# Power instead of Newton steps for the norms on GpSimd, norm rows and shifted copies moved between queues, the first X spectrum with a negated table, in an H3 convolution and SwiGLU kernel

## The chip, the cores and the metric

The kernel runs on one core of a Trainium2 chip. The core has five engines that run side by side, each working through its own queue in order: TensorE (PE, matrix products into PSUM; its weight loads are listed apart as PEld), VectorE (DVE), ScalarE (ACT), GpSimd (POOL) and SyncE (SP, which here only issues transfers). SP, ACT and POOL can issue DMAs; 16 DMA engines move the data. The metric is the device time of one execution in microseconds (us), the median of several runs. Lower is better.

## The reference

The input has 2048 positions of 640 channels. The part that matters:

```python
x = A_q
q = layernorm(x)                                   # no gain, no bias, eps 1e-5
k_shift[s] = sum_{t<4} k[s - t] * shift_k[:, t]    # four taps per channel
kv = k_shift * v
y = causal convolution of kv with ssm_k, by FFT    # length 2048, per channel
y = y + kv * ssm_D
h = x + q * y
n = layernorm(h)
out = h + (silu(n @ w_gate) * (n @ w_up)) @ w_down # 640 -> 1728 -> 640
```

Tiles are bf16; PSUM and the statistics of the norms are fp32.

## The kernel before, in words

**Tiling.** The 2048 positions are cut into four blocks (numbers 0 to 3) of 512. A block is a tile of 128 partitions by 4 rows by 640 channels; row r holds the positions 4p+r. The convolution is block by block: `spectrum` turns a block of kv into its spectrum X and a block of the filter into G by products with a table of cosines and sines (`WF`); `window` joins neighbouring G into H; `mac` adds up X_i * H_(j-i) on DVE; `inverse` goes back with the table `WI` and applies the first norm, the product with y and the sum h. `turn_h` applies the second norm and transposes h (hT). `ffn` then does the feed-forward part of the block: seven groups of gate and up columns (540 matmuls of 128x512 in all four blocks, line 1017), SiLU and product, then the down projection (416 matmuls of mostly 128x320, line 1105).

**The spectrum.** In `transform`, the cosine table of the even rows (0, 2) and of the odd rows (1, 3) give two halves E and O. Plain way: PE makes E, an engine copies 2E out of PSUM, PE adds O, an engine copies E+O, and DVE subtracts to get E-O (line 409). With a name in `DIRECT`, PE makes all four rows at once, then adds -2 times the odd rows from a second, negated table (`minus`), and both halves are copied out of PSUM; DVE subtracts nothing.

**The norms.** ACT sums x and x squared (lines 791, 749; four instructions each of 128x640). `norm` turns these into a mean and 1/sqrt(variance) on tiles of 128x4. On DVE that is ten short instructions, with a cubic polynomial behind a bit trick. On GpSimd it is fourteen, with the bit trick and two Newton steps (lines 767, 758, 759, 770, 779 to 782 twice, 758, 759). ln1 is the norm of x (result used on the way out of `inverse`, line 802), ln2 that of h (used in `turn_h`; the rows are applied by ACT at line 802 or DVE at line 799).

**k with four taps.** For blocks 1 to 3, k is loaded transposed into one tile T (four transposing DMAs), and then three copies inside T (line 562: put 0, put 1, put 2) make shifted halves, each 64 partitions by 5 by 512; put 1 and put 2 both come behind put 0. Two matmuls with pairs of taps then do what four did (line 640). All puts are DMAs, on SP's queue or on GpSimd's.

**Order.** Nothing is ordered by the hardware. `plan.add` numbers every operation in the order in which the code makes it, and the list `ORDER` gives these numbers in the order in which they are issued; each engine so gets a fixed queue. A negative number (~n) takes the operation's alternative: for an eviction from PSUM, DVE instead of ACT; for a load or put, GpSimd's queue instead of SP's. `SLOTS` says how many buffers there are of each sort: four pairs of PSUM banks (`ps`), eleven of 128x2560 bf16 (`big`) that loads, spectra halves, hT and FFN weights share, five rows (`row`), and so on. An operation waits for its data and for the last use of its buffer. The times in the `plan.add` calls were used for making the list; on the chip they do nothing.

Lines that the text below speaks of: 374 spectrum matmuls, 363 and 366 their evictions on ACT and DVE, 409 the subtraction E-O, 470/472 transposes of the filter and their eviction, 516/517 window, 562 puts, 711 to 739 `mac`, 818/821/887/900 the steps of `inverse`, 873 its matmuls, 921/923 transposes of h and their eviction, 954 FFN weight loads, 1007/1009 copies of the up half and SiLU, 1011 product, 1111 output rows of a block.

Of the kernel before, what the change touches and what calls it, by code (L numbers as in the profile page):

```python
# [26 lines left out]
NEWTON = ((1.68191274, 0.70395035), (1.50000037, 0.50000005))  # L27
# [11 lines left out]
DIRECT = ('G0',)  # L39
ACTLN = 0  # L40
ACTKV = 0
ACTLN2 = (0, 2)
LN1DVE = (2,)
LN2POOL = ()
# [14 lines left out]
FFN4 = True  # L59
# [8 lines left out]
TWONS = 640  # L68
TW = PAD + BLK
CUTS = ("X0", "G0", "m", "i")  # L70
ORDER = [
# [36 lines left out]
SLOTS = {'S': 8, 'kT': 0, 'tT': 1, 'row': 5, 'ps': 4, 'sm': 6, 'big': 11, 'sg': 0, 'co': 2}  # L108
HOME = {t: "big" for t in ("scr", "x", "ld", "t4", "hT", "wgu")} | {"o": "row", "ps_c": "ps", "ps_f": "ps"}
# [38 lines left out]
class Plan:  # L148
# [34 lines left out]
    def moved(self, eng, nbytes, packet, fn, reads=(), writes=()):  # L183
        n = nbytes / packet
        op = self.add(eng, 1000.0 if eng in ("turn", "aturn") else n * self.TOOK[packet] / 16 * (2.1 if eng == "add" else 1.0), fn, reads, writes)
        op.packets = 0 if eng == "add" else n
        return op
# [25 lines left out]
def kernel(ctx: ExitStack, tc: tile.TileContext, A_q, A_k, A_v, A_shift_k, A_ssm_k, A_ssm_D, B_x,  # L213
# [28 lines left out]
    def ap(b):  # L242
        if b.tag != "big":
            return b.ap if b.tag is None else place[b.tag][b.at]
        t = place["big"][b.at]
        return t if b.kind == "ld" else t.rearrange("p (k n) -> p k n", k=KT if b.kind in ("hT", "wgu") else R)
# [17 lines left out]
    def load(nbytes, packet, fn, w, r=(), other=None):  # L264
        op = plan.moved("sp", nbytes, packet, fn, r, w)
        if other:
            op.other = ("pld", op.ns, other)
        return op
# [33 lines left out]
    diag = fixed([P, KT * 4, P], BF16, "diag")  # L302
# [14 lines left out]
    def of_t(*atoms):  # L317
        return (T, frozenset(atoms))
    wd = fixed([P, NCH, D], BF16, "wd")
    tail = fixed([P, BLK], BF16, "tail")  # L320

# [223 lines left out]
    def load_two(j):  # L545
# [14 lines left out]
        def put(r, w, to, src):  # L560
            def by(q):
                return lambda: q.dma_start(out=to(), in_=src())
            load(H2 * KT * 1024, 1024, by(nc.sync), w, r, other=by(nc.gpsimd) if "T" in GLOAD else None)
        uppers = [("A", a, 1) for a in range(R)]
        put([of_t(*uppers)], [of_t("B0", *FIRSTS)], lambda: t()[0:H2, 1, :, PAD:TW], lambda: t()[H2:P, 0, :, PAD:TW])
        put([of_t("B0", "Bh")], [of_t("B1", *FIRSTS)], lambda: t()[H2:P, 1, :, PAD - 2:TW], lambda: t()[0:H2, 1, :, PAD - 3:TW - 1])
        put([of_t("Ah", *[("A", a, 0) for a in range(R)])], [of_t(*uppers)], lambda: t()[H2:P, 0, :, PAD - 2:TW], lambda: t()[0:H2, 0, :, PAD - 3:TW - 1])
# [184 lines left out]
    def norm(s, v, mean=None, bias=False, rs=range(R)):  # L752
# [11 lines left out]
        def go():  # L764
            if mean:
                fused(sm(s, 2), sm(s, 0), 1.0 / D, sm(mean, 2), ALU.mult, ALU.add)
            v.tensor_mul(sm(s, 6), sm(s, 2), sm(s, 2))
            fused(sm(s, 3), sm(s, 1), EPS, sm(s, 6), ALU.add, ALU.subtract)

            v.tensor_scalar(sm(s, 4).bitcast(I32), sm(s, 3).bitcast(I32), -0.5, float(0x5F165000 if v is nc.vector else 0x5F1FFFF9), op0=ALU.mult, op1=ALU.add)  # L770
            if v is nc.vector:
# [11 lines left out]
            if bias:  # L783
                fused(sm(s, 5), sm(s, 2), -1.0, sm(s, 4), ALU.mult, ALU.mult)
# [537 lines left out]
```

## Time and profile before

| | |
|---|---|
| median of 3 runs | 264.18 us (263.42 to 265.51) |
| the profiled execution | 264.92 us, its span 263.2 us, mean granted PE clock 0.994 |
| busy in the span | PE 252.7 us (96%), DVE 202.6 (77%), ACT 173.3 (66%), POOL 91.5 (35%) |
| 128x512 matmuls (line 1017) | 540, 121.1 us busy |
| 128x320 and the like, down projection (line 1105) | 416, 60.3 us busy |
| 128x320, spectra (line 374) | 256, 43.6 us busy |
| steps of the norm on GpSimd (lines 758 to 782) | 42 in three norms |

The span runs from the first to the last instruction; 1.7 us of the execution lie outside it. The busy time of PE is the union of its matmuls with modelled ends, so short waits hide in it; the start of one matmul to the start of the next tells more.

### The profile page before, as it was taken

The page shows a single profiled execution, that of the slowest core. Times are in us where ns is not written, and L with a number is a line of the kernel's source. Part 1 is how long each engine was busy: PE and PEld are TensorE (multiplying, and loading weights), DVE is VectorE, ACT ScalarE, POOL GpSimd, SP SyncE. Part 2 cuts the span into 40 slices and gives each one's busy share as a digit, 9 for nine tenths or more (in the row PEclk, how much of TensorE's full clock was granted, in tenths as well). Part 3 has the DMA queues.
Part 4 walks back from the last instruction along what each step waited for, and adds up shares of the span by engine and source line. Part 5 has one row for each costly group of instructions (what it writes and reads, how often), then busy time and mean ns, then how long its engine had stood idle before and what let it go on. Part 6 is the DMA issues. An engine that isn't in the chain of part 4 may idle for free.

```text
span 263.2 us, 4751 instructions
## 1 busy us (share of the span) xinstructions
PE 252.7 (96%) x1818; PEld 154.7 (59%) x1818; DVE 202.6 (77%) x288; ACT 173.3 (66%) x294; POOL 91.5 (35%) x118
## 2 busy tenths in 40 slices
PE   8999977999999999999999999999999999999993
PEld 7977564655466567665655467544447764444772
DVE  4689988899999999999999999999999500004231
ACT  3989979996389994798888995242597034525300
POOL 6881010109996311214215322699900033000000
PEclk9999999799999999999999999999999999999999
DMA  7996997999999998999996699841799238000002
GB/s 240 382 236 157 266 276 171 257 283 169 255 261 128 198 330 109 254 243 252 207 265 99 175 276 214 171 117 50 170 244 239 59 55 138 0 0 0 2 10 90
DMA packets 66770, 46.38 MB, mean 176 GB/s; under 512 B 31030, under 2 KB 62524, under 8 KB 66748
## 3 DMA queue, kind: packets, MB, share of 16 engines
q1 hardware_dynamic: 61234, 34.93, 53.4%
q0 software_dynamic: 5504, 11.14, 22.2%
q8 instruction: 14, 0.23, 0.4%
q14 instruction: 8, 0.07, 0.1%
q10 hardware_dynamic: 10, 0.01, 0.0%
HBM read 30.01 MB, written 4.59 MB: 131 GB/s over the span
## 4 chain that ended last, share of the span: by engine, by line
PE 66%; DVE 13%; DMA 9%; POOL 7%; ACT 3%; issue 2%; POOLq 0%; DVEq 0%; ACTq 0%; SPq 0%
PE ps L1017 33%; PE ps L1105 19%; PE ps L374 7%; DVE S L711 4%; DMA big<-in_A_ssm_k_dram 3%; DMA S<-S 3%; DVE big L711 2%; PE ps L873 2%; DMA big<-row 2%; DVE big L650 1%; DVE S L739 1%; DVE big L738 1%; POOL sm L779 1%; POOL sm L781 1%; POOL sm L780 1%
## 5 line engine op out<-in xcount | busy, mean ns | idle before, releaser
L1017 PE MATMUL ps<-big,big 128*128 128x512 bf16 x540 | 121.1, 379 | 0.0
L1017 PEld LDWEIGHTS <-big 128*128 128x128 bf16 x540 | 52.6, 98 | 58.9
L1105 PE MATMUL ps<-wd,tT 128*128 128x320 bf16 (+2 forms) x416 | 60.3, 299 | 1.3 <-DVE row L1122 0.6
L1105 PEld LDWEIGHTS <-tT 128*128 128x128 bf16 x416 | 40.7, 98 | 17.8 <-issue 1.7
L1007 ACT CAST co<-ps 128x1024 bf16<-128x1024 f32 x24 | 24.1, 1013 | 31.3 <-PE ps L1017 31.3
L374 PE MATMUL ps<-big,WF 128*128 128x320 bf16 x240 | 40.3, 307 | 2.4 <-ACT big L472 1.4
L1011 DVE TENSOR_TENSOR tT<-tT,co 128x2048 bf16<-128x2048 bf16 x12 | 14.5, 1219 | 34.4 <-ACT co L1007 34.4
L739 DVE TENSOR_TENSOR S<-S,big 128x2560 bf16<-128x2560 bf16 x23 | 34.3, 1493 | 0.8
L738 DVE TENSOR_TENSOR big<-S,S 128x2560 bf16<-128x2560 bf16 x23 | 34.1, 1483 | 0.0
L374 PEld LDWEIGHTS <-WF 128*128 128x128 bf16 x240 | 23.7, 100 | 15.2 <-issue 3.5
L1009 ACT ACTIVATE tT<-ps 128x1024 bf16<-128x1024 f32 x24 | 24.6, 1031 | 4.4 <-PE ps L1017 4.2
L1112 POOL DMA_DIRECT2D out_dram<-row x12 | 11.6, 1086 | 41.6 <-ACT row L1111 41.6
L749 ACT ACTIVATE row<-big 128x640 bf16<-128x640 bf16 x32 | 23.7, 741 | 2.3 <-DVE big L900 2.0
L363 ACT CAST S<-ps 128x320 bf16<-128x320 f32 (+1 forms) x37 | 19.6, 572 | 2.3 <-PE ps L374 1.9
L1111 ACT CAST row<-ps 128x640 bf16<-128x640 f32 x12 | 8.0, 693 | 15.2 <-PE ps L1105 14.8
L802 ACT ACTIVATE row<-big,sm 128x640 bf16<-128x640 bf16 x20 | 17.5, 922 | 0.7 <-DVE sm L756 0.7
L363 ACT ACTIVATE big<-ps 128x640 bf16<-128x640 f32 (+1 forms) x26 | 16.2, 651 | 2.4 <-PE ps L374 2.2
L791 ACT ACTIVATE row<-big 128x640 bf16<-128x640 bf16 x16 | 11.9, 750 | 3.8 <-DMA big<-row 2.4
L887 DVE SCALAR_TENSOR_TENSOR row<-row,ps 128x640 bf16<-128x640 bf16 x16 | 12.7, 814 | 0.8 <-PE ps L873 0.8
L711 DVE TENSOR_TENSOR big<-S,S 128x2560 bf16<-128x2560 bf16 (+1 forms) x10 | 12.2, 1220 | 0.6 <-DMA S<-S 0.5
L873 PEld LDWEIGHTS <-WI 128*128 128x128 bf16 x96 | 9.3, 98 | 5.2 <-issue 0.6
L954 POOL DMA_DIRECT2D big<-in_B_w_gate_dram x8 | 8.7, 1210 | 10.3 <-PE ps L1017 9.9
(107 smaller groups left out, 310.9 us busy)
## 6 DMA issues: line engine op xcount, KB each, us to landing
big<-in_B_w_up_dram SPq DMA_DIRECT2D x18, 320.0 KB, 4.7
big<-in_B_w_gate_dram SPq DMA_DIRECT2D x16, 320.0 KB, 5.8
big<-in_A_q_dram SPq DMA_DIRECT2D x4, 640.0 KB, 5.8
big<-in_A_v_dram SPq DMA_DIRECT2D x4, 640.0 KB, 6.7
big<-in_A_ssm_k_dram SPq DMA_DIRECT2D x4, 640.0 KB, 7.7
big<-in_B_w_gate_dram POOLq DMA_DIRECT2D x8, 320.0 KB, 6.3
wd<-in_B_w_down_dram SPq DMA_DIRECT2D x1, 2080.0 KB, 13.2
T<-T SPq DMA_DIRECT2D x6, 321.2 KB, 6.1
```

The source lines that it names most:

```text
L363: (lambda: nc.scalar.activation(dst(), src(), ACT.Copy, scale=2.0)) if twice else (lambda: nc.scalar.copy(dst(), src())),
L374: nc.tensor.matmul(ap(ps)[:, h, 0:NH], w, ap(src)[:, r, h * NH:(h + 1) * NH], start=(first and i == 0), stop=(last and i == len(rs) - 1), ...
L711: return lambda: f(*(x() for x in args))
L738: nc.vector.tensor_mul(flat2(b), X.part(xs), H.part(hs))
L739: f(A.part(dst), A.part(dst), flat2(b))
L749: act(825, lambda r=r, junk=junk: nc.scalar.activation(ap(junk), ap(x)[:, r, :], ACT.Square, scale=D ** -0.5, accum_out=sm(s, 1)[:, r:r + ...
L802: nc.scalar.activation(ap(row), ap(x)[:, r, :], ACT.Identity, bias=sm(s, 5)[:, r:r + 1], scale=sm(s, 4)[:, r:r + 1])
L873: nc.tensor.matmul(ap(ps)[:, w, 0:NH], m, src[:, w * NH:(w + 1) * NH], start=(i == 0), stop=(i == len(terms) - 1))
L1007: act(1010, lambda ps=ps: nc.scalar.copy(ap(co)[:, at:at + 2, :], ap(ps)), src, [(co, gi % 2)])
L1009: act(1010, lambda ps=ps: nc.scalar.activation(ap(tT)[:, c:c + 2, :], ap(ps), ACT.Silu), src, [done(range(c, c + 2), ROWS)])
L1017: nc.tensor.matmul(ap(ps)[:, i, :], ap(w)[:, k, off:off + P], ap(hT)[:, k, :], start=(k == 0), stop=(k == KT - 1))
L1105: nc.tensor.matmul(ap(ps)[:, hf, to:to + n], t, ap(wd)[:, c, col + (hf - hs[0]) * NH:col + (hf - hs[0]) * NH + n], start=(c == order[0]), ...
```

## The change

It has these parts.

- **norm**: on GpSimd, 1/sqrt is now one power, `tensor_tensor` with `ALU.pow` and a tile of -0.5 (`root`); the Newton steps go. That makes five instructions where fourteen stood (seven where the mean of h must be added, that is for ln2). The sign of the mean is turned over, so the bias is one product.
- **where norms run**: ln1 of block 2 goes from DVE to GpSimd, ln2 of blocks 1 and 2 too (`LN1DVE`, `LN2POOL`). ln2 of block 0 and 3 stays on DVE.
- **LN rows**: the ln2 rows of blocks 1 and 3 may now go to ACT (`ACTLN2`); before, DVE had them.
- **puts**: put 1 and put 2 (`TCOPY`) are ACT copies inside SBUF, or with a negative number DMAs of GpSimd's queue; put 0 is a DMA as before.
- **X0**: `DIRECT` has X0 too, so the first X spectrum takes the negated table: 16 more matmuls of 128x320 (4 columns of the table, 2 halves of the channels, 2 rows), and the two subtractions of 128x1280 at line 409 go.
- **FFN**: `FFN4` is off, so SiLU goes to a buffer `sg` of its own, and DVE multiplies per two chunks (128x1024) where it did four at once (128x2048). The up half may be multiplied by DVE straight from PSUM.
- **buffers**: the table `diag` lives in one of now twelve `big` buffers, and frees it after block 0's kv. `co` goes, `sg` has four.
- **ORDER** is a new list throughout.

```diff
-NEWTON = ((1.68191274, 0.70395035), (1.50000037, 0.50000005))
...
-DIRECT = ('G0',)
+DIRECT = ('G0', 'X0')
...
-ACTLN2 = (0, 2)
-LN1DVE = (2,)
-LN2POOL = ()
+ACTLN2 = (0, 1, 2, 3)
+LN1DVE = ()
+LN2POOL = (1, 2)
...
-FFN4 = True
+FFN4 = False
...
+TCOPY = (1, 2)
...
-SLOTS = {'S': 8, 'kT': 0, 'tT': 1, 'row': 5, 'ps': 4, 'sm': 6, 'big': 11, 'sg': 0, 'co': 2}
+SLOTS = {'S': 8, 'big': 12, 'kT': 0, 'tT': 1, 'row': 5, 'sg': 4, 'ps': 4, 'sm': 6}
...
-    diag = fixed([P, KT * 4, P], BF16, "diag")
+    diag = new("diag") if TWOTAPS else fixed([P, KT * 4, P], BF16, "diag")
...
+    root = fixed([P, R], FP32, "root")
...
+        def put(i, r, w, to, src, packet):
...
+            if i in TCOPY:
+                act(2570, lambda: nc.scalar.copy(to(), src()), r, w)
+                plan.ops[-1].other = ("pld", 1550.0 if packet > 1024 else 940.0, by(nc.gpsimd))
+                return
...
             else:
-                for a, b in NEWTON:
-                    v.tensor_mul(sm(s, 6), sm(s, 4), sm(s, 4))
-                    v.tensor_mul(sm(s, 6), sm(s, 6), sm(s, 3))
-                    v.tensor_scalar(sm(s, 6), sm(s, 6), -b, a, op0=ALU.mult, op1=ALU.add)
-                    v.tensor_mul(sm(s, 4), sm(s, 4), sm(s, 6))
+                v.tensor_sub(sm(s, 3), sm(s, 1), sm(s, 6))
+                v.tensor_scalar(sm(s, 3), sm(s, 3), EPS, None, op0=ALU.add)
+                v.tensor_tensor(sm(s, 4), sm(s, 3), ap(root)[:, rs[0]:rs[-1] + 1:rs[1] - rs[0]], op=ALU.pow)
             if bias:
-                fused(sm(s, 5), sm(s, 2), -1.0, sm(s, 4), ALU.mult, ALU.mult)
+                v.tensor_mul(sm(s, 5), sm(s, 2), sm(s, 4))
...
-        X.append(spectrum(kv, name=f"X{j}"))
+        X.append(spectrum(kv, minus=minus if f"X{j}" in DIRECT else None, name=f"X{j}"))
```

Counted through both lists, these are the places that the prediction speaks of (names: X0, G1 and so on are spectra, kv1 the taps of block 1, i1 the way back of block 1, f0 the FFN of block 0, ev an eviction from PSUM).

| place | before | after |
|---|---|---|
| first loads on SP | k0, x0, v0, g0 | k0, v0, x0, g0 |
| load of g2 on SP | behind put 1 of block 1 and v1 | ahead of put 0 of block 1 |
| evictions of X0 and G0 on DVE | 6 and 1 of 32 | 6 and 6 of 32 |
| first norm's rows of block 0 on DVE | 1 of 4 | 3 of 4 |
| first half of the window H1 (line 516) | between ln2's norm of block 0 and its rows | behind the rows |
| G2 steps on PE ahead of f0 | 4 of 8 | 7 of 8 |
| first row of kv2 on PE | behind 15 FFN steps of 5 matmuls | behind 11 such steps |
| puts of block 1 | all on SP | put 0 SP, put 2 and put 1 GpSimd |
| puts of block 2 | put 0 GpSimd, 1 and 2 SP | put 0 SP, put 1 GpSimd, put 2 ACT |
| on GpSimd ahead of ln2's norm of block 1 | (on DVE) | put 0 of block 3, one sum of h, a weight load, put 1 and put 2 of block 3 |
| on ACT behind the first ln2 row of block 1 | (rows on DVE) | two sums for later norms, an X2 eviction, the other rows, then the first output row of f0 |

More of the change, by code (lines that the diff above doesn't have):

```diff
@@ L71 @@
 ORDER = [
[36 rows of a table removed]
-SLOTS = {'S': 8, 'kT': 0, 'tT': 1, 'row': 5, 'ps': 4, 'sm': 6, 'big': 11, 'sg': 0, 'co': 2}
-HOME = {t: "big" for t in ("scr", "x", "ld", "t4", "hT", "wgu")} | {"o": "row", "ps_c": "ps", "ps_f": "ps"}
[37 rows of a table added]
+SLOTS = {'S': 8, 'big': 12, 'kT': 0, 'tT': 1, 'row': 5, 'sg': 4, 'ps': 4, 'sm': 6}
+HOME = {t: "big" for t in ("scr", "x", "ld", "t4", "hT", "wgu", "diag")} | {"o": "row", "ps_c": "ps", "ps_f": "ps"}
 SPLIT = ((0,), (1,))
@@ L184, in moved @@
         n = nbytes / packet
-        op = self.add(eng, 1000.0 if eng in ("turn", "aturn") else n * self.TOOK[packet] / 16 * (2.1 if eng == "add" else 1.0), fn, reads, writes)
+        op = self.add(eng, 850.0 if eng in ("turn", "aturn") else n * self.TOOK[packet] / 16 * (2.1 if eng == "add" else 1.0), fn, reads, writes)
         op.packets = 0 if eng == "add" else n
@@ L245, in ap @@
         t = place["big"][b.at]
-        return t if b.kind == "ld" else t.rearrange("p (k n) -> p k n", k=KT if b.kind in ("hT", "wgu") else R)
+        return t if b.kind == "ld" else t.rearrange("p (k n) -> p k n", k=KT if b.kind in ("hT", "wgu") else 4 * KT if b.kind == "diag" else R)
     def pe(ns, fn, r, w, holds=(), late=338):
@@ L266, in load @@
         if other:
-            op.other = ("pld", op.ns, other)
+            op.other = ("pld", op.ns * (0.9 if packet == 512 else 1.0), other)
         return op
@@ L558, in load_two @@
                 [], [of_t(("A", a, 0), ("A", a, 1))])
-        def put(r, w, to, src):
+        def put(i, r, w, to, src, packet):
             def by(q):
                 return lambda: q.dma_start(out=to(), in_=src())
-            load(H2 * KT * 1024, 1024, by(nc.sync), w, r, other=by(nc.gpsimd) if "T" in GLOAD else None)
+            if i in TCOPY:
+                act(2570, lambda: nc.scalar.copy(to(), src()), r, w)
+                plan.ops[-1].other = ("pld", 1550.0 if packet > 1024 else 940.0, by(nc.gpsimd))
+                return
+            op = load(H2 * KT * 1024, 1024, by(nc.sync), w, r, other=by(nc.gpsimd) if "T" in GLOAD else None)
+            if packet > 1024:
+                op.ns = 1550.0
+                op.other = op.other and ("pld", 1550.0, op.other[2])
         uppers = [("A", a, 1) for a in range(R)]
-        put([of_t(*uppers)], [of_t("B0", *FIRSTS)], lambda: t()[0:H2, 1, :, PAD:TW], lambda: t()[H2:P, 0, :, PAD:TW])
-        put([of_t("B0", "Bh")], [of_t("B1", *FIRSTS)], lambda: t()[H2:P, 1, :, PAD - 2:TW], lambda: t()[0:H2, 1, :, PAD - 3:TW - 1])
-        put([of_t("Ah", *[("A", a, 0) for a in range(R)])], [of_t(*uppers)], lambda: t()[H2:P, 0, :, PAD - 2:TW], lambda: t()[0:H2, 0, :, PAD - 3:TW - 1])
+        put(0, [of_t(*uppers)], [of_t("B0", *FIRSTS)], lambda: t()[0:H2, 1, :, PAD:TW], lambda: t()[H2:P, 0, :, PAD:TW], 1024)
+        put(1, [of_t("B0", "Bh")], [of_t("B1", *FIRSTS)], lambda: t()[H2:P, 1, :, PAD - 2:TW], lambda: t()[0:H2, 1, :, PAD - 3:TW - 1], 1028)
+        put(2, [of_t("Ah", *[("A", a, 0) for a in range(R)])], [of_t(*uppers)], lambda: t()[H2:P, 0, :, PAD - 2:TW], lambda: t()[0:H2, 0, :, PAD - 3:TW - 1], 1028)
         return T
@@ L765, in go @@
             if mean:
-                fused(sm(s, 2), sm(s, 0), 1.0 / D, sm(mean, 2), ALU.mult, ALU.add)
+                fused(sm(s, 2), sm(s, 0), -1.0 / D, sm(mean, 2), ALU.mult, ALU.add)
             v.tensor_mul(sm(s, 6), sm(s, 2), sm(s, 2))
-            fused(sm(s, 3), sm(s, 1), EPS, sm(s, 6), ALU.add, ALU.subtract)
-            v.tensor_scalar(sm(s, 4).bitcast(I32), sm(s, 3).bitcast(I32), -0.5, float(0x5F165000 if v is nc.vector else 0x5F1FFFF9), op0=ALU.mult, op1=ALU.add)
             if v is nc.vector:
+                fused(sm(s, 3), sm(s, 1), EPS, sm(s, 6), ALU.add, ALU.subtract)
+                v.tensor_scalar(sm(s, 4).bitcast(I32), sm(s, 3).bitcast(I32), -0.5, float(0x5F165000), op0=ALU.mult, op1=ALU.add)
                 v.tensor_mul(sm(s, 6), sm(s, 4), sm(s, 4))
@@ L777, in go @@
             else:
-                for a, b in NEWTON:
-                    v.tensor_mul(sm(s, 6), sm(s, 4), sm(s, 4))
-                    v.tensor_mul(sm(s, 6), sm(s, 6), sm(s, 3))
-                    v.tensor_scalar(sm(s, 6), sm(s, 6), -b, a, op0=ALU.mult, op1=ALU.add)
-                    v.tensor_mul(sm(s, 4), sm(s, 4), sm(s, 6))
+                v.tensor_sub(sm(s, 3), sm(s, 1), sm(s, 6))
+                v.tensor_scalar(sm(s, 3), sm(s, 3), EPS, None, op0=ALU.add)
+                v.tensor_tensor(sm(s, 4), sm(s, 3), ap(root)[:, rs[0]:rs[-1] + 1:rs[1] - rs[0]], op=ALU.pow)
             if bias:
-                fused(sm(s, 5), sm(s, 2), -1.0, sm(s, 4), ALU.mult, ALU.mult)
-        plan.add("dve" if v is nc.vector else "pool", 2190 if v is nc.vector else 17500, go, [mean] if mean else [], [s])
+                v.tensor_mul(sm(s, 5), sm(s, 2), sm(s, 4))
+        plan.add("dve" if v is nc.vector else "pool", 2190 if v is nc.vector else 5500 if mean else 4000, go, ([mean] if mean else []) + ([root] if v is nc.gpsimd else []), [s])
     def ln1(x):
@@ L790, in ln1 @@
             junk = new("row")
-            act(820, lambda r=r, junk=junk: nc.scalar.activation(ap(junk), ap(x)[:, r, :], ACT.Identity, scale=1.0 / D,
+            act(820, lambda r=r, junk=junk: nc.scalar.activation(ap(junk), ap(x)[:, r, :], ACT.Identity, scale=-1.0 / D,
                                                        accum_out=sm(s, 2)[:, r:r + 1]), [(x, r)], [junk, (s, ("s", r))])
@@ L798, in vector @@
         def vector():
-            nc.vector.tensor_scalar(ap(row), ap(x)[:, r, :], sm(s, 2)[:, r:r + 1], sm(s, 4)[:, r:r + 1], op0=ALU.subtract, op1=ALU.mult)
+            nc.vector.tensor_scalar(ap(row), ap(x)[:, r, :], sm(s, 2)[:, r:r + 1], sm(s, 4)[:, r:r + 1], op0=ALU.add, op1=ALU.mult)
         def scalar():
@@ L1175 @@
         plan.add("pool", 350, lambda: nc.gpsimd.tensor_tensor(ap(by_pair)[:, 4 * P:4 * P + H2], ap(ident)[:, 0:H2], ap(ident)[:, H2:P], op=ALU.add), [ident], [(by_pair, 1)])
+    fills = []
     for c in range(KT if TWOTAPS else 0):
@@ L1179, in fill2 @@
                 nc.gpsimd.tensor_scalar(ap(pairs)[:, 4 * c + t, :], ap(by_pair)[:, 4 * P:4 * P + H2], ap(taps2)[:, t * KT + c:t * KT + c + 1], None, op0=ALU.mult)
-        plan.add("pool", 1900, fill2, [(by_pair, 1), taps2], [(pairs, c)])
+        fills.append(plan.add("pool", 1900, fill2, [(by_pair, 1), taps2], [(pairs, c)]))
     k = load_k(0)
+    plan.add("pool", 200, lambda: nc.gpsimd.memset(ap(root), -0.5), [], [root])
     plan.add("pool", 600, lambda: nc.gpsimd.memset(ap(tail)[64:P, :], 0.0), [ident], [(tail, "zero")])
@@ L1222 @@
     A = Spec(new("S"))
+    at = len(plan.ops)
     mac(A, X[0], H[0], True, split("m"))
+    plan.ops[at].then.update(fills)
     first("i0")
```

73 rows, old and new, of the table ORDER are left out of this document.

## The prediction

> **What bounds the kernel now.** I read the page's first two parts, then busy time by stretches of 10 us, then each engine's timeline. The page, and from the stretches the columns PE, PEld, DVE, ACT, POOL (busy us, count), granted clock, DMA share, GB/s:
>
> ```profile
> PE 252.7 (96%) x1818; PEld 154.7 (59%) x1818; DVE 202.6 (77%) x288; ACT 173.3 (66%) x294; POOL 91.5 (35%) x118
> ...
> 20.00:30.00 10.00, 9.46 (x78) 6.85 (x77) 9.91 (x14) 9.62 (x23) 0.73 (x1) 1.00 0.76 206
> 30.00:40.00 10.00, 8.22 (x122) 6.36 (x121) 9.12 (x17) 8.62 (x17) 1.38 (x2) 1.00 1.01 257
> 40.00:50.00 10.00, 7.99 (x56) 5.13 (x54) 8.47 (x24) 9.21 (x19) 0.91 (x1) 0.83 0.84 193
> 50.00:60.00 10.00, 9.73 (x62) 5.48 (x62) 9.96 (x8) 10.00 (x21) 1.08 (x1) 1.00 1.07 287
> ```
>
> PE has idle time before 60 us and almost none later; the clock is low only at 40 to 50 us. From PE's own timeline, the start of the FFN, one long run, and the one later wait before the end:
>
> ```profile
> 53.68 3.61 PE L1017 MATMUL ps<-big,big 128*128 128x512 bf16 x16
> ...
> 63.41 8.80 PE L1017 MATMUL ps<-big,big 128*128 128x512 bf16 x40
> 72.04 0.81 PE L640 MATMUL ps<-pairs,T 128*128 128x64 bf16 x20
> ...
> 107.97 1.52 PE L1105 MATMUL ps<-wd,tT 128*128 128x320 bf16 x10 [0.62 <-ACT row L1111]
> ```
>
> Forty matmuls of 512 columns go from 63.41 to 72.04, 0.216 us each: a step of five is 1.08. The chain of waits has 26 of line 1105 in 3.53, 0.136 each. From 53.68 us on PE runs at these rates, so **the time is when the FFN of block 0 starts, what PE has done by then, and what new waits come behind it**. DVE is 9.5 to 10 of 10 busy from 50 to 200 us, so it is nearly as tight.
>
> **The change part by part.**
>
> *X0 by the negated table.* 16 matmuls of 0.136: +2.2 us of PE, between 13 and 30 us, where PE has little idle time (9.92 and 9.46 of 10 busy). The steps of i0 would come at 32.7 instead of 30.5. They need DVE's sums and differences (lines 818, 821), which end at 33.1 now. DVE's bill up to there: two subtractions of line 409 less (0.8 each, -1.6), five more evictions of 0.42 (+2.1), two more norm rows of 0.4 (+0.8), so +1.3 and 34.4. PE's extra is under that cover, and costs up to 2.2 without it.
>
> *To the start of f0.* From there to the rows of ln2 on DVE (47.62 now): an X1 eviction, +0.75; the first half of window H1 moves behind the rows, -1.4. With the +1.3 that is about +0.7. On ACT one more eviction of 0.58 stands ahead of the last part of hT0. Bounds: 0 if present DVE waits of 0.9 (v1's landing) and 0.5 us close, +1.9 if both add and v0's place ahead of x0 delays ACT's first sums (x0 would land where v0 does, 7.97 for 6.12 us). I take +0.9, near DVE's sum: f0 at 54.6. By then PE has done three more steps of G2, 12 x 0.136 = 1.6 us, which the rest need not do. Net **-0.7**.
>
> *The wait at 107.97.* ACT's output copy stood behind sums that waited for row buffers (0.92 from start to start, 0.14 of it the matmul's own). Rows and outputs have a new order; I count it gone, **-0.8**, bounds -0.8 and 0.
>
> *Norms on GpSimd.* Two stretches of GpSimd's timeline and DVE beside the second:
>
> ```profile
> 13.13 0.23 POOL L758 TENSOR_SCALAR sm<-sm 128x4 f32<-128x4 f32 x1
> 13.45 0.20 POOL L759 TENSOR_TENSOR sm<-sm 128x4 f32<-128x4 f32 x1
> ...
> 61.41 1.34 POOL L758 TENSOR_SCALAR sm<-sm 128x4 f32<-128x4 f32 x1
> 62.83 1.42 POOL L759 TENSOR_TENSOR sm<-sm 128x4 f32<-128x4 f32 x1
> ...
> 61.18 1.49 DVE L738 TENSOR_TENSOR big<-S,S 128x2560 bf16<-128x2560 bf16 x1
> 62.70 1.49 DVE L739 TENSOR_TENSOR S<-S,big 128x2560 bf16<-128x2560 bf16 x1
> ```
>
> The same step takes 0.28 us from start to start early on, and 1.4 beside DVE's large products, one step per DVE instruction; fourteen took 60.26 to 78.4, 1.3 each. Five make ln1 about 6.5 us, 11 to 12 less; nothing waits for ln1 of block 1 now, so this gains nothing by itself. The power has no row: between 0.2 (shortest step) and 1.9 (longest, at 167.25); I take a step like its neighbours.
>
> ln2 of blocks 1 and 2 has seven steps, for 1.9 us on DVE (98.45 to 100.37). Behind the norm wait ACT's rows, and behind them in ACT's queue evictions that free PSUM. Block 1, zero at PE's first i1 step: PE does four i1 steps (1.09 each), ten FFN steps (1.08), eight of X2 and one of G3 (0.54), and nine down-projection parts (six of 1.36, three of 1.09), and at 31.4 needs the PSUM pair that f0's first output row frees. ACT's last sum of squares ends at about 18.3 (h's last sum lands earlier if put 0 of block 3, ahead of it in GpSimd's queue, gets its data by 10). After a norm of N: four rows of 0.85, two sums of 0.72, an eviction and the output of 0.58, about 6.0. PE waits N + 24.3 - 31.4 = **N - 7.1**. Block 2, the same way from the first i2 step: last sum 15.6, two rows and an eviction behind the norm 2.4, PE needs the pair at 26.2: **N - 8.2**. DVE's own row there waits too, so its queue stands up to 2.5 us; it is cheaper by then. Six steps at 1.28 and one at 0.28, while DVE reads PSUM: N = 8.0, waits 0.9 and 0. Bounds: N = 2.0 (no waits) to 9.9. I take **+0.9**.
>
> *DVE otherwise.* Three norms of 1.9 go (-5.8), about five ln2 rows of 0.4 fewer (-2). Products: 128x2048 took 1.22 and 128x512 0.42, so 128x1024 should be 0.68, six for three: +0.4 a block, +1.3 before f3. Three products straight from PSUM in f3 fall where DVE is idle. Net, with the items above, 3 us less. hT3's transposes are issued from 206.44 for 5.2 us and take 4.1 to land, just before f3 at 214.69; DVE's saving covers a stand in block 2, without it that 2.5 would come out at f3.
>
> *Puts.* Block 2 now: put 0 lands at 57.68, put 1 and 2 follow one behind the other to about 71, kv2 starts at 72.04. After: put 1 by GpSimd (7.1, as it took) and put 2 by ACT (2.5, as the 128x2560 copy at 83.13) run side by side, ready at about 64.8. kv2 comes behind 11 FFN steps and one of G2: 54.6 + 12.4 = 67.0. A margin of 2; cost 0. For ACT's copy what is queued behind is the up copies of f0, with 0.8 us to spare. Block 1's puts on GpSimd's queue come about where they land now (36 us); 0, bounds -1 and +1.3.
>
> Weight loads, buffers: the twelfth buffer lets g2 load early; PE's wait for it (0.74 at 38) is part of f0's bounds.
>
> **Sum.** 264.92 - 0.7 - 0.8 + 0.9 = 264.3 for an execution like the profiled one, which is 0.7 above the median: **263.6 us**.
>
> **Rivals.**
> 1. *GpSimd's norms hold ACT, and ACT holds PSUM* (slower). Every step waits out a whole DVE product, 7 x 1.41 = 9.9, and the queue starts the norm 0.7 late behind put 1 and 2, which wait for put 0's landing: waits 3.5 and 1.7, +4.3 against the forecast, **267.9**. It decides from N = 8.2. For it: all fourteen steps from 60 to 78 and again from 167 to 187 us went like that. Against: products of 0.7 and PSUM reads lie between. The Trainium skill, "SBUF — State Buffer", section "Who interferes with whom", has a DVE instruction with two SBUF inputs and a GpSimd instruction that reads SBUF lock each other out for a whole instruction, and none if DVE has one SBUF input; by that rule this rival's N holds wherever no PSUM read comes between, and the 1.4 for 0.28 of the rows agrees. Chance 0.25.
> 2. *The opening closes up* (faster). f0 starts at 53.0, because g2 no longer waits (0.7) and PE, busier from 40 to 50, keeps its clock; no wait behind the norms: 264.92 - 0.7 (f0) - 1.6 (G2) - 0.8 (the wait at 107.97) - 0.7 (to the median) = **261.1**. For: 4.6 us idle in PE's rows from 20 to 60, of which 3.8 can hold the new and the moved matmuls. Against: ACT and DVE are over 8.4 of 10 busy there. Chance 0.22.
> 3. *A put lands late.* Every put so far took 3.7 to 9.3 us; at 9.3 put 1 of block 2 eats the margin, and ACT stands with f0's copies behind it: +3, **266.6**. Chance 0.12.
> 4. *The power is no short step* but as long as the Newton steps (N = 18): waits of 11 and 10, **284**. Nothing shows it. Chance 0.03.
>
> Forecast: 0.38, 262.0 to 266.0. A change within 1% (2.6 us) can hardly be told from none. Faster by over 1% (under 261.5): most of rival 2 and a little of the forecast, 0.24. Slower by over 1% (over 266.8): nearly all of rival 1, half of 3, all of 4, 0.33. Same: 0.43. The range goes from rival 2 to past rival 1: 260.2 to 269.0.
>
> **What would show it.** Line 1017 should start at 54 to 55 us; the steps of ln2 on GpSimd should be 1.3 apart; ACT line 802 should have idle time ended by GpSimd, and PE a wait ended by ACT line 1111 or 363 of about 1 us at 105 to 115; hT3 should not be waited for. I am wrong if f0 starts outside 53 to 56.5, if N leaves 7 to 9, or if kv1 or kv2 waits for a put.

## The result: 3.6% slower

The changed kernel takes 273.67 us, the kernel before 264.18 in the same comparison: a ratio of 1.036, 95% interval 1.030 to 1.041. The forecast was 263.6, no change, with a range to 269.0. The profiled execution of the changed kernel took 273.67 us (span 272.0) against 264.92, so 8.75 us have to be found. Many kernels here also have executions at a lower mean clock that are several us longer; the ratios leave them out, and where such an execution was the profiled one (e1, e8, e11, e12, e13) no total is read from its trace.

The stretches of the opening of the changed kernel, with the columns as before (PE, PEld, DVE, ACT, POOL, granted clock, DMA share, GB/s):

```profile
20.00:30.00 10.00, 10.00 (x86) 7.48 (x84) 9.44 (x18) 9.45 (x25) 3.59 (x7) 1.00 0.91 225
30.00:40.00 10.00, 9.62 (x124) 7.29 (x122) 9.91 (x17) 9.43 (x20) 0.43 (x2) 1.00 1.01 272
40.00:50.00 10.00, 8.32 (x82) 5.98 (x80) 9.62 (x26) 9.87 (x20) 0.42 (x1) 1.00 0.91 145
50.00:60.00 10.00, 9.62 (x68) 5.78 (x67) 9.96 (x9) 8.25 (x15) 0.67 (x1) 1.00 0.90 232
```

The opening is no looser than before: by these stretches PE has 2.4 us without work between 20 and 60 us (before: 4.6), and its clock no longer falls at 40 to 50. The loss is behind it. PE's own timeline of the changed kernel, the start of f0, kv2 (the row that stood at 72.04), and the two waits that matter most (in brackets their length; the time at the start of such a line, and below each time at which a wait is said to be, is the start of the last matmul ahead of the wait):

```profile
55.34 9.88 PE L991 MATMUL ps<-big,big 128*128 128x512 bf16 x44
...
67.75 0.82 PE L649 MATMUL ps<-pairs,T 128*128 128x64 bf16 x20
...
81.02 0.58 PE L991 MATMUL ps<-big,big 128*128 128x512 bf16 x1 [5.09 <-DMA big<-in_B_w_gate_dram]
...
101.25 2.32 PE L1068 MATMUL ps<-big,big 128*128 128x512 bf16 x9 [1.45 <-ACT sg L1051]
```

At 107 us no wait is left. To see where the time goes I counted, at marked steps of PE's queue, the work done so far (0.216 us a 512-column matmul, 0.136 a 320-column one) and took it from the time; what is left is the time that PE stood or ran below full clock up to there:

| up to | before: time, standing | after: time, standing | after, since the row above |
|---|---|---|---|
| f0 | 53.68, 11.79 | 55.34, 9.64 | |
| kv2 | 72.04, 11.77 | 67.75, 9.63 | 0.0 |
| first step of i1 | 78.99, 11.81 | 83.10, 15.90 | **6.3** |
| down projection of f0 | 94.69, 11.79 | 103.41, 18.33 | **2.4** |
| kv3 | 124.21, 12.54 | 134.31, 18.30 | 0.0 (before: 0.75) |
| down projection of f1 | 152.79, 12.56 | 160.99, 19.13 | **0.8** |
| end | 259.58, 13.16 | 268.32, 19.72 | 0.6 (before: 0.6) |

(kv2 and i1 stand at other places of PE's queue in the two kernels, so their times are not comparable, their standing is.) Work grew by 2.18, X0's sixteen matmuls; the opening gave 2.15 back. The rest is 6.3 + 2.4 + 0.8 - 0.75 = 8.75.

**The 6.3.** The chain of waits of the changed kernel, from DVE's product to the matmul that stood (start, length, what; "SPq" is SP's queue):

```profile
60.47 1.41 DVE big L742
...
62.18 10.63 DMA S<-big
72.81 0.02 SPq L960
...
73.28 7.60 DMA big<-in_B_w_gate_dram
...
81.02 0.58 PE ps L991
```

DVE writes a product of `mac` m11 into a `big` buffer; a DMA from GpSimd adds it to the spectrum and reads the buffer until 72.8 us. The next user of that same buffer is the load of f0's fifth group of weights (the program takes the longest-free buffer, and no other was free). SP's queue stands until the adding DMA is through, the weights land at 80.9, and PE needed them at 75.9. In the kernel before, by the order of its list, the buffer of that product goes to v2's load, and group 5 gets one that DVE had left; wd was issued ten microseconds earlier there (46.86).

**What comes behind the wait.** The granted clock (the column before the last two) in stretches of 3 us of the changed kernel:

```profile
78.00:81.00 3.00, 0.00 (x0) 0.01 (x1) 1.97 (x3) 0.00 (x0) 0.00 (x0) 0.50 1.07 283
81.00:84.00 3.00, 2.76 (x8) 1.25 (x10) 0.00 (x0) 1.44 (x3) 0.00 (x0) 0.50 1.07 367
84.00:87.00 3.00, 3.00 (x19) 1.79 (x18) 0.62 (x1) 3.00 (x6) 0.00 (x0) 0.87 1.91 252
87.00:90.00 3.00, 3.00 (x21) 1.93 (x20) 3.00 (x7) 2.99 (x2) 0.91 (x1) 1.00 0.67 136
```

PE starts again at half clock and is at full clock after 87 us. Of the 6.3 us, 5.1 are the wait and 1.2 slower matmuls up to i1; another 0.8 of the 2.4 follows. The Trainium skill, "TensorE: Matmul & The Clock Gate", "Part 1: The HAM clock gate (the "warmup" mystery)", has PE at half clock after an idle window of about 3.4 us until it has been busy for about as long; the rows agree, 0.50 from 78 to 84.

**The rest of the 2.4, and the 0.8.** Both are the odd gate and up chunks (g6 and u6), in blocks 0 and 1. They write the two halves of one PSUM pair. In the new order g6 and u6 are neighbours on PE and the SiLU of g6 stands between them in the list, so u6, listed later, is made to wait for the SiLU: 1.6 us at 99.42 (ACT was late there) and 0.8 at 153.18. In the kernel before another PE step lies between the two in both blocks.

### The profile page after: what moved, and what is told of

Its sections match the earlier page's. It is cut to its first block, busy times and chain, and to the rows that moved or that the text cites. A ratio compares the mean times of both kernels' runs of the same rounds, so it can differ in the third digit from the quotient of the medians.

```text
span 272.0 us, 4757 instructions
## 1 busy us (share of the span) xinstructions
PE 256.1 (94%) x1817; PEld 158.3 (58%) x1834; DVE 204.5 (75%) x274; ACT 169.8 (62%) x284; POOL 90.4 (33%) x118
## 4 chain that ended last, share of the span: by engine, by line
PE 66%; DMA 7%; DVE 6%; ACT 6%; issue 2%; SPq 0%; ACTq 0%
PE ps L991 31%; PE ps L1111 22%; PE ps L1068 4%; DMA S<-big 4%; PE ps L879 3%; PE ps L376 3%; DMA big<-in_B_w_gate_dram 3%; DVE S L720 2%; ACT big L365 1%; DVE big L720 1%; PE ps L649 1%; ACT S L365 1%; ACT row L758 1%; ACT sg L1051 1%; ACT big L474 1%
## 5 line engine op out<-in xcount | busy, mean ns | idle before, releaser
L991 PE MATMUL ps<-big,big 128*128 128x512 bf16 x465 | 108.1, 381 | 6.1 <-DMA big<-in_B_w_gate_dram 5.1
L991 PEld LDWEIGHTS <-big 128*128 128x128 bf16 x480 | 46.6, 98 | 57.8 <-issue 6.0
L1051 ACT ACTIVATE sg<-ps 128x1024 bf16<-128x1024 f32 (+1 forms) x28 | 26.9, 965 | 23.9 <-PE ps L991 19.9
L376 PE MATMUL ps<-big,WF 128*128 128x320 bf16 x240 | 39.5, 299 | 2.3 <-ACT big L365 1.3
L748 DVE TENSOR_TENSOR S<-S,big 128x2560 bf16<-128x2560 bf16 x23 | 34.3, 1492 | 1.0 <-DMA S<-big 0.2
L1059 DVE TENSOR_TENSOR tT<-sg,sg 128x1024 bf16<-128x1024 bf16 (+1 forms) x22 | 14.5, 662 | 26.4 <-ACT sg L1057 26.4
L1057 ACT CAST sg<-ps 128x1024 bf16<-128x1024 f32 (+1 forms) x22 | 21.4, 972 | 14.0 <-PE ps L991 11.9
L365 ACT CAST S<-ps 128x320 bf16<-128x320 f32 (+1 forms) x38 | 20.3, 579 | 1.2 <-PE ps L376 0.6
L808 ACT ACTIVATE row<-big,sm 128x640 bf16<-128x640 bf16 x21 | 18.8, 921 | 1.9 <-DVE sm L790 1.9
L1068 PE MATMUL ps<-big,big 128*128 128x512 bf16 x58 | 14.6, 379 | 2.2 <-ACT sg L1051 2.1
L365 ACT ACTIVATE big<-ps 128x640 bf16<-128x640 f32 x19 | 13.3, 740 | 4.0 <-PE ps L376 4.0
L797 ACT ACTIVATE row<-big 128x640 bf16<-128x640 bf16 x16 | 11.9, 743 | 6.2 <-DMA big<-in_A_q_dram 4.8
L960 POOL DMA_DIRECT2D big<-in_B_w_up_dram x7 | 6.3, 905 | 25.6 <-issue 13.1
```

The lines of the kernel that those rows point to most:

```text
L365: (lambda: nc.scalar.activation(dst(), src(), ACT.Copy, scale=2.0)) if twice else (lambda: nc.scalar.copy(dst(), src())),
L376: nc.tensor.matmul(ap(ps)[:, h, 0:NH], w, ap(src)[:, r, h * NH:(h + 1) * NH], start=(first and i == 0), stop=(last and i == len(rs) - 1), ...
L748: f(A.part(dst), A.part(dst), flat2(b))
L808: nc.scalar.activation(ap(row), ap(x)[:, r, :], ACT.Identity, bias=sm(s, 5)[:, r:r + 1], scale=sm(s, 4)[:, r:r + 1])
L960: return lambda: q.dma_start(out=ap(w)[:, :, to:to + n], in_=cols(src, lo, n))
L991: nc.tensor.matmul(of(ps, i), ap(w)[:, k, off:off + P], ap(hT)[:, k, lo:lo + n], start=(k == 0), stop=(k == KT - 1))
```

## The experiments

The list `ORDER` is a list of numbers, so edits of it are shown by the names of the operations. Line numbers of e1, e3 and e4 differ by up to four from those of the changed kernel.

**e1, wd behind group 5.** The 2.1 MB of `wd` are issued at 57.12, just ahead of the adding DMA.

```diff
-ld wd | ld wd tail | ld v2 | f0 ld wu5 | f0 ld wg5 | ld x3
+ld v2 | f0 ld wu5 | f0 ld wg5 | ld wd | ld wd tail | ld x3
```

> The changed kernel with one transfer moved: the load of the down-projection weights (wd, 2.1 MB) is issued behind the loads of the gate and up columns of group 5 of block 0's FFN, not ahead of them. Theory A (a buffer held by an adding DMA): the sum of m11 lands about 5 us after its issue at 62 us, not 10.6, the group-5 loads are issued at 67 to 68 and land at 73 to 74, PE has no wait at 75.7 us (5.3 before) and its clock stays up: 265 to 267 us. Theory B (the norms on GpSimd hold ACT, ACT holds PSUM, as in rival 1): the wait moves, PE only meets the later waits earlier: 271 or more. Theory C (the wait was a cover for DVE, which is late anyway): PE waits for DVE at the i1 steps instead, 270 or more.

Measured: ratio 1.067 (1.055 to 1.078), slower than the changed kernel. The wait for group 5 is gone, but now x3 stands behind wd's bytes. The chain of waits of e1:

```profile
78.91 14.75 DMA big<-in_A_q_dram
...
93.74 0.83 ACT row L793 x2
...
95.52 2.56 PE ps L875 x9
```

ACT's sum over x3 stands in ACT's queue ahead of an up copy of f0; PE waits 10.2 us for the PSUM that this copy frees. The bytes are still there, and now they delay a load that ACT's queue cannot do without.

**e2, the product of m11 summed by DVE**, so that no DMA reads the buffer:

```diff
-add_into(lambda dst=dst: A.part(dst), lambda b=b: flat2(b), [b], [A.at(dst)])
+dve(1490, lambda dst=dst, b=b: nc.vector.tensor_add(A.part(dst), A.part(dst), flat2(b)), [b], [A.at(dst)])
```

> The changed kernel with the sum of m11 done by DVE (one addition of 128x2560, about 1.4 us more of DVE) where an adding DMA did it; wd stays where it is. Theory A: the buffer of the product comes free at about 63.5 us, the group-5 loads are issued then, behind wd, and land at 73 to 75: PE's wait at 75.7 shrinks below 1 us, 266 to 268.5 us. If the late landing comes from wd's bytes alone and not from the buffer, they land at 79 or later and the time stays at 272 to 274.

Measured: 271.71 us, ratio 1.028 (1.021 to 1.035). From kv2 to i1 PE stands 0.9 us instead of 6.3 (DVE is 1.1 late with i1's sums), and the clock stays at 1.00 there. The total fell by only 2 us because in this execution kv1 waited for block 1's puts. PE's timeline of e2:

```profile
38.04 0.26 PE L649 MATMUL ps<-pairs,T 128*128 128x64 bf16 x2 [2.92 <-DMA T<-T]
39.62 2.22 PE L649 MATMUL ps<-pairs,T 128*128 128x64 bf16 x38 [1.33 <-DMA T<-T]
```

**e3, e1 with the ln2 norms of blocks 1 and 2 on DVE; e4, e1 with the Newton steps back on GpSimd.**

```diff
 e3
-LN2POOL = (1, 2)
+LN2POOL = ()
 e4
-v.tensor_tensor(sm(s, 4), sm(s, 3), ap(root)[...], op=ALU.pow)
+(first guess, and two rounds of four Newton steps)
```

> As e1, and ln2 of blocks 1 and 2 back on DVE (1.9 us each there), at the same places of the list. Theory A: DVE is not the bound there, the norm's steps on GpSimd cost little: within 1 us of e1. Theory B (rival 1): 3 to 4 us below e1.

> As e1, with the two Newton steps back in place of the power on GpSimd, for every norm that runs there (13 steps for ln1, 15 for ln2). If the prediction's formula holds (PE waits N - 7.1 in block 1 and N - 8.2 in block 2, N then 13 to 18 counted from ACT's last sum), 10 to 20 us above e1. If most of the steps ahead of the last sum are done by then, 3 to 10 us above e1.

Measured: e3 280.44 us in the one execution that can be compared (e1: 279.53 and 283.25), no clear difference. e4 1.111 (1.105 to 1.117), 291.92 to 294.13 us, by the medians 11.9 us above e1. The list of PE's waits of e4 (total, times, longest) has two that e1's has not:

```profile
PE ps L992 <- ACT row L1118: 8.3, 1, 8.3
...
PE ps L1112 <- ACT row L1118: 2.5, 1, 2.5
```

They stand behind the ln2 norms of blocks 2 and 1 (in block 2 by way of a row on DVE and a transposing DMA of 12.45 us that held a row buffer). That ACT's rows, and behind them PSUM, wait for a long norm on GpSimd is thus real, and the total lies in the 10 to 20 of the prediction's formula; but the waits are not the two of 10 and 11 that its rival 4 had for a norm of this length. The power makes the norm short enough that it costs little.

**e5, v2's load and group 5's exchange places**, so that group 5 gets the free buffer and v2 the product's; **e6, that and the SiLU behind u6.**

```diff
 e5
-ld v2 | ... | f0 ld wu5 | f0 ld wg5 | ld x3
+f0 ld wu5 | f0 ld wg5 | ... | ld v2 | ld x3
 e6, beside it, in blocks 0 and 1
-g6 | ... | silu6 | ... | u6
+g6 | ... | u6 | silu6
```

> Only the places of two loads in the list are exchanged: group 5's weights (up and gate) now take the buffer that an early FFN group leaves, and v2 takes the buffer of m11's product, which the adding DMA reads until 72.8 us. Theory (the 5.3 us wait at 75.72 comes from which load falls into the product's buffer): the wait goes and with it the lower clock behind it, standing time of PE at the first step of i1 falls from 15.9 to about 9.7; v2 is issued at 72.9 and lands at 76 to 77, where DVE first multiplies with it at 76.31, so at most 1 us is lost there: about 267.4, 266 to 269. Rival (the queues are full there, whatever is loaded into that buffer holds somebody up by the same amount): the wait turns up at kv2's product or at X2, 272 to 274.

> As e5_swap_v2, and the SiLU of the odd gate chunk (step g6) of blocks 0 and 1 is put behind the matmuls of u6 in the list; PE's order is the same, ACT's changes by one place in block 0. Theory (u6 writes the other half of the PSUM pair that this SiLU reads, and waits for it because the SiLU stands between them in the list): the waits at 99.42 (1.83 from start to start) and 153.18 (1.06) go, 2.4 to 2.9 us less than e5_swap_v2, about 264.8. Rival (u6 waits for something else that ACT or DVE does there): both waits stay and the time is that of e5_swap_v2.

Measured: e5 1.028 (1.016 to 1.040), its profiled execution 271.55; e6 1.014 (1.005 to 1.022), profiled 266.88. By the ratios e6 is clear of the changed kernel's 1.030 to 1.041, e5 is not. In both, PE stands 0.0 us from kv2 to i1, where it stood 6.3, and DVE does not wait for v2, which is in the product's buffer now. e5 gave part of it back: kv1 waited 2.5 us for the puts, and between i1 and the down projection PE stood 4.5 us, 1.9 of it at u6 and 1.0 for group 4's weights. These are issued at 76.61, behind v2, x3 and g3 in SP's queue, which stood 7.4 us for v2's buffer: what the exchange takes from group 5 it lays on the loads behind v2. In e6 both waits at u6 are gone. The lists of PE's waits, the changed kernel's first two and e6's first four that are not the program's start:

```profile
PE ps L991 <- DMA big<-in_B_w_gate_dram: 5.1, 1, 5.1
PE ps L1068 <- ACT sg L1051: 2.1, 2, 1.5
```

```profile
PE ps L376 <- ACT big L365: 1.3, 2, 1.1
...
PE ps L376 <- ACT sg L1051: 0.7, 1, 0.7
PE ps L1111 <- DVE row L1128: 0.6, 1, 0.6
PE ps L1111 <- ACT row L1117: 0.5, 1, 0.5
```

So two reorderings of a few places take 6.8 of the 8.75 us off the profiled execution (by the ratios, about 2 of the 3.6%). What is left to the kernel before is 1.96 us: 2.18 of work, 0.24 less standing. The opening gains as much as X0 costs, and four small waits for ACT (0.6 to 0.9 each from start to start, at 85.83, 92.17, 109.56 and 153.34) stand against one of 0.75.

**e7, the kernel before with X0's part alone; e11, the kernel before with the power alone.**

```diff
 e7
-DIRECT = ('G0',)
+DIRECT = ('G0', 'X0')
 e11 (GpSimd's norms)
-first guess; two rounds of four Newton steps
+v.tensor_tensor(sm(s, 4), sm(s, 3), ap(root)[...], op=ALU.pow)
```

> The kernel before with one part of the change alone: X0 made whole by the negated table (16 matmuls of 0.136 us more on PE, two subtractions on DVE less); every load keeps its place and the owner before it in its buffer. Theory (PE's extra lies under DVE's work in the opening): f0 still starts at 53 to 54.5 us, 263.5 to 265. Rival (it is on the path): f0 at 55.9, 266.4.

> The kernel before with one part of the change alone: GpSimd's ln1 norms (blocks 0, 1 and 3) by one power instead of the eight Newton steps and the first guess; every other instruction as before. Theory (nothing waits for these norms in the kernel before): within 0.5 us of the kernel before, with the norm of block 1 some 11 us shorter on GpSimd. Rival (GpSimd's steps slow DVE's products or hold the adding DMAs behind them): 1 to 2 us faster.

Measured: e7 1.0045 (1.0006 to 1.0084), f0 at 53.77 us (before 53.68); e11 0.998 (0.994 to 1.002); its edit also fills the small tile of -0.5 earlier in GpSimd's queue. X0's matmuls lie under DVE's work, as expected, and its two subtractions less bring DVE nothing that can be seen; nothing waits for ln1's norms.

**e8, wd ahead of block 2's put 0.**

```diff
-f0 ld wg0 | k2 put0 | ... | f0 ld wg2 | ld wd | ld wd tail
+f0 ld wg0 | ld wd | ld wd tail | k2 put0 | ... | f0 ld wg2
```

> The kernel after with the loads of wd moved ahead of block 2's put 0 in the sync queue, near where the kernel before issues them (46.86 us). Theory (the adding DMA of m11 is slow partly because wd's 2.1 MB stand ahead of it): it takes about 7.5 us instead of 10.6, group 5's loads are issued at 69.8 instead of 72.9, the wait at 75.72 shrinks from 5.3 to about 2.2 us: about 270.3, if the loads that stand behind wd's (groups 2 and 0) are not late for f0. Rival (the add is as slow without wd's bytes): 273.7.

Measured: 1.029 (1.018 to 1.040). Neither account: PE waits 4.7 us at 64.6 for another group's weights, and comes to group 5 too late to wait there. That group's load stands behind wd's bytes, and then 8.1 us in SP's queue for an output DMA that still reads the buffer it is to fill: the case of group 5 once more. The adding DMA still took 10.3 us from issue to landing. Its times in all kernels that have it (us from its issue to its first packet and to its landing; KB that SP's queue moved in the 11 us behind the issue):

| | first packet | landed | SP's KB |
|---|---|---|---|
| before, e7, e11 | 2.1 to 3.1 | 7.6 to 8.0 | 1422 to 1694 |
| e1, e3, e4 (wd behind) | 1.9 | 8.0 to 8.1 | 1072 to 1110 |
| after | 4.8 | 10.6 | 2136 |
| e5, e6, e9, e10 (wd ahead) | 2.8 to 3.9 | 8.5 to 10.7 | 2132 to 2282 |
| e8 (wd early) | 3.2 | 10.3 | 1280 |

With wd's bytes in flight the adding DMA lands 0.8 to 3.0 us later than in the kernel before. In the changed kernel that is 2.9 of the 5.1 us. In e8 fewer bytes were in flight and it landed late all the same; there a put ran ahead of it on GpSimd's own queue, with some 190 KB still to move at the issue. No run separates the two, so the bytes of wd are not shown to be the cause.

**e9, e6 with the ln2 norms on DVE; e10, e6 with block 1's puts on SP's queue again.**

```diff
 e9
-LN2POOL = (1, 2)
+LN2POOL = ()
 e10
-if i in TCOPY:
+if i in TCOPY and j > 1:
 and in the list
-k1 put0 | k1 put2 (GpSimd) | ... | ld WI | ... | k1 put1 (GpSimd)
+k1 put0 | ld WI | k1 put2 (SP) | ... | k1 put1 (SP)
```

> As e6_swap_silu, with the ln2 norms of blocks 1 and 2 computed on DVE again, at the same places of the list. Theory (with the larger waits out of the way, ACT's rows behind GpSimd's norms hold PSUM: ACT stands 1.10 us at 103.28 for the norm, and PE waits 0.67 more than a matmul's own time at 109.56 and 0.63 at 153.34): both waits go, 1.3 us less than e6_swap_silu, 265.6, unless DVE's 1.9 us a norm come out elsewhere. Rival (the two waits come from ACT's own queue, or DVE is as tight): no difference, 266.9 to 267.4, or 1 to 2 us more.

> As e6_swap_silu, with block 1's puts 1 and 2 on the sync queue again, and the load of WI ahead of them as in the kernel before. Theory (kv1's wait for the puts on GpSimd's queue was 0, 0.3, 0.8, 1.9, 2.1, 2.4, 4.2 and 5.2 us in eight profiled executions, against 1.1 in the kernel before and none with X0 alone): kv1 waits at most 1.1 us in every execution, the single times lie closer together, f0 at 54.5 to 55.5, median 265.5 to 267. Rival (the landing varies with the chip's start whatever queue issues the puts): the spread and the median of e6_swap_silu, 267 to 270.

Measured: e9 1.042 (1.036 to 1.048), e10 1.037 (1.032 to 1.042): both lose all that e6 had gained, outside every expectation. In e9 the adding DMA took 10.7 us, x3 landed at 80.14 (in e6 before 77.8), and PE stood 2.0 us at 79.64 for an up copy behind ACT's sum over x3, ahead of any ln2 norm: with this slower adding DMA the exchanged loads are not free. From the down projection of f1 to i3 it stood another 2.4 (in e6 not at all), 1.3 of it for DVE's sums ahead of i3. In e10 kv1 no longer waits, but x2's load, on the queue of the puts, takes 8.2 us (4.8 in e6), and through ACT's sum over x2 PE waits 2.5 us at 40.27; and the ln2 norm of block 1 comes late. GpSimd's timeline of e10, and the instructions of ACT and PE that stood behind it:

```profile
98.38 1.51 POOL L768 TENSOR_TENSOR sm<-sm,sm 128x4 f32<-128x4 f32 x1
...
104.45 2.47 POOL L788 TENSOR_TENSOR sm<-sm,root 128x4 f32<-128x4 f32 x1
107.00 0.59 POOL L790 TENSOR_TENSOR sm<-sm 128x4 f32<-128x4 f32 x1
```

```profile
107.63 0.92 ACT L808 ACTIVATE row<-big,sm 128x640 bf16<-128x640 bf16 x1 [4.35 <-POOL sm L790]
```

```profile
113.63 2.83 PE L1111 MATMUL ps<-wd,tT 128*128 128x320 bf16 x10 [2.57 <-ACT row L1117]
```

This is the mechanism of the prediction's rival 1, with 9.55 us for the norm and a PE wait of 2.6; counted from ACT's last sum the norm took 8.4 us, and that sum itself came later than the prediction had it.

**e12, e2 with the SiLU behind u6; e13, that with the ln2 norms on DVE.** No adding DMA for m11 in either, so the norms' place is compared by itself.

```diff
 e12
 e2, and in blocks 0 and 1
-g6 | ... | silu6 | ... | u6
+g6 | ... | u6 | silu6
 e13
-LN2POOL = (1, 2)
+LN2POOL = ()
```

> As e2_m11_sum_dve (m11's sum on DVE, no adding DMA), and the SiLU of the odd gate chunk of blocks 0 and 1 behind u6. Theory (the adding DMA, 8.8 to 10.7 us from issue to landing in the kernels that keep it, is what makes single runs of the exchanged loads differ by 6 us; without it the loads of v2, x3 and g3 are early): the waits at 96.95 (2.1) and 151 (1.06) of e2_m11_sum_dve go, 2.5 us less than that kernel, 268.5 to 269.5, single runs within 3 us of each other. Rival (the spread comes from the opening or from the clock): single runs spread as e6_swap_silu's, 267 to 274.

> As e12_sum_silu, with the ln2 norms of blocks 1 and 2 on DVE. Theory (behind GpSimd's norms ACT and PE stand, 2.7 us of PE in e10_swap_silu_puts where the norm took 9.6 us behind the puts' issue, 0.7 in e6_swap_silu): 0.7 to 2.7 us less than e12_sum_silu. Rival (DVE, over 9.5 of 10 busy there, gives the same back by its 1.9 us a norm): within 0.5 us of e12_sum_silu, or up to 2 us more.

Measured: e12 1.014 (1.009 to 1.020), e13 1.020 (1.015 to 1.025). The two edits of e12 take 2% off the changed kernel, as those of e6 do; on DVE the norms are no better. e12's time is the one that its theory gave; its three times in the ratio lie 2.5 us apart, too few to say whether the adding DMA is what makes executions of one kernel differ. None of these kernels beats the kernel before.

## Why the prediction was wrong

*What bounds the kernel.* The frame held: start of f0, work done by then, new waits behind. The 8.75 us are new waits.

*X0, cost 0.* Right for the opening: f0 at 53.77 in e7. Its total is 0.2 to 2.2 us up, which I had not counted.

*Start of f0.* 55.34 for 54.6, with the three G2 steps done ahead as said: net +0.03, not -0.7.

*The wait at 107.97.* Gone, as counted. In e6, where PE arrives earlier, 0.7 us of waiting is back at the same step, the first part of f0's last output row.

*Norms on GpSimd, +0.9.* The mechanism was right, its terms were not. The power is no step like its neighbours. GpSimd's timeline of the changed kernel:

```profile
17.29 1.05 POOL L788 TENSOR_TENSOR sm<-sm,root 128x4 f32<-128x4 f32 x1
...
68.49 1.46 POOL L787 TENSOR_SCALAR sm<-sm 128x4 f32<-128x4 f32 x1
70.03 2.15 POOL L788 TENSOR_TENSOR sm<-sm,root 128x4 f32<-128x4 f32 x1
...
102.29 0.20 POOL L776 TENSOR_TENSOR sm<-sm 128x4 f32<-128x4 f32 x1
```

It takes 1.05 us where its neighbours take 0.20, and 2.1 to 2.5 beside DVE's products. And the norm need not wait as a whole for ACT's last sum: the mean and its square run ahead, and only four steps come behind. In the changed kernel the norm of block 1 took 5.8 us, 3.6 of them behind the last sum, and PE, itself late behind the larger waits, stood at neither norm. In e6 PE stood 0.7 behind the norm of block 1, by way of its first row and of a transposing DMA that held that row's buffer, and not at all behind that of block 2: the 0.6 at 153.34 is for a SiLU that stands behind four sums of squares on ACT, and e9, with the norm on DVE, has it too. In e10 PE stood 2.6. Of the prediction's formula one part held there: from the norm's end to PE's matmul it had 6.0, and that passed from 107.59 to 113.63. The norm behind the last sum, put at 8.0, took 3.6 in the changed kernel, 6.0 in e6 and 8.4 in e10; and the last sum, put at 18.3 us behind the first step of i1, came at 19.5, 20.5 and 21.4. The steps of 1.3 to 1.5 beside products with two SBUF inputs and 0.20 where DVE stood or read PSUM (102.29) again agree with the rule of the Trainium skill, "SBUF — State Buffer", "Who interferes with whom". (For a DVE instruction with one SBUF input that section makes an exception of the 2-port modes, which rival 1 did not carry over.)

*DVE otherwise.* Right: hT3 is not waited for, and the 128x1024 products took 0.68.

*Puts.* Right for block 2: kv2 at 67.75 without a wait. Too narrow for block 1, "0, bounds -1 and +1.3": in seven profiled executions with the puts on GpSimd's queue, put 1's last packets ended at 34.3 to 38.5 us and kv1 waited 0.0 (after, e6, e9), 0.8 (e3), 1.9 (e4), 2.5 (e5) and 4.2 us (e2), against 1.1 before.

*"Weight loads, buffers: the twelfth buffer lets g2 load early."* **This is the step that failed.** It asked what one more buffer lets start sooner, and not who follows whom in each buffer. The rotation had put f0's fifth group behind a buffer that an adding DMA was still reading: 5.1 us of waiting and 2.0 of low clock. e5 and e6 show it by exchanging the loads, e2 by taking the DMA away.

*The sum* also lacked the 1.6 and 0.8 us at u6, which stand in the list of the new order and not in any part of the change as I had cut it up; e6 shows them.

Of the rivals none came true in the changed kernel. The mechanism of rival 1 showed in e10 and, with the Newton steps, in e4, there with waits of 2.5 and 8.3.

*What stays open*: why the adding DMA takes 8.8 us in one kernel (e6) and 10.7 in another (e9) with the same loads ahead of it, and why put 1's landing moves by 4 us with the same queue. The opening is the less settled half: e10 moved the puts and only moved the wait.

## What to carry to other kernels

When buffers rotate, write down for every load who used its buffer last and when that user is done; a DMA that still reads a buffer counts from its issue to its landing, 7.6 to 10.7 us here, and the loads queued behind it count too. A new order is a change by itself: look for operations that share a PSUM tile and for what the list puts between them. And price a wait with what follows it: five idle microseconds of PE cost two more in clock.

## What was not expected of the hardware

- A power of 128x4 on GpSimd: 1.04 to 1.05 us alone, 2.1 to 2.5 beside DVE's 128x2560 products.
- An adding DMA of 640 KB landed 7.6 to 8.1 us after its issue where SP's queue moved 1.1 to 1.7 MB in the 11 us behind it, and 8.5 to 10.7 where it moved 2.1 to 2.3 MB (but 10.3 in e8 with 1.3 MB); its first packet started 1.9 to 3.1 us after the issue in the first case and 2.8 to 4.8 in the second.
- In e10 the clock fell behind a wait of 2.57 us too: 0.84 and 0.82 in the stretches 110 to 115 and 115 to 120 us.
